# Fifteen small SBUF copies in a fused attention and MLP kernel, issued from ScalarE instead of SyncE

## The chip, the cores and the metric

The kernel runs on one core of a Trainium2 chip. The metric is the device time of one execution, in microseconds (us); runs of the kernel before and of the changed kernel are compared by their medians. Besides the runs there is one profiled execution of the kernel before, read through its profile: busy time by engine, a timeline of instructions, the chain of work that ended last, and the waits.

The engines are named as in the profile: PE is TensorE (matmuls), ACT is ScalarE, DVE is VectorE, POOL is GpSimd, SP is SyncE. SPq and ACTq stand for instructions that the sequencer of SP or of ACT carries out itself: DMA issues and separate semaphore waits.

## What is computed

One layer of 2048 positions and 448 channels: a windowed attention of 16 heads (28 channels each) in which each position looks at 8 earlier positions in steps of 2, and then a mixing MLP, each with a layer norm ahead and a residual.

```python
x = A_x
h = x + _A_ref(_layernorm(x), A_wqkv, A_wo)       # attention, 8 keys per query: idx = pos - 2*w
h2 = h + _B_ref(_layernorm(h), B_w1, B_w2, B_w3, B_w4)

# inside _A_ref
vg = v[:, :, idx_c, :].reshape(B, H, S, W, Dh)
logits = jnp.einsum("bhsd,bhswd->bhsw", q, kg) * scale
attn = _softmax(jnp.where(mask, logits, -1e9))
o = jnp.einsum("bhsw,bhswd->bhsd", attn, vg)
return o.reshape(B, S, D) @ wo
```

`_B_ref` multiplies the normalized input with w1, applies gelu, shifts four channel groups by -1, 1, -2 and 2 positions, multiplies with w2, adds the residual, normalizes again and applies a second two-layer MLP (w3, gelu, w4).

## The kernel before

The sequence is worked on in four blocks t = 0 to 3 of 512 positions. A block passes through phases: N1 (layer norm), A1 (q and k, transposed), V (v), A2 and S (logits by elementwise products on DVE and reducing matmuls on PE, then softmax), A3 (the weighted sum of v), O (output matmul and residual), B1 (norm and w1). The second half runs B2 (w2), W3 and B3 over units of 3, 4, 4, 4 and 1 tiles of 128 positions.

**How v reaches A3.** Phase V makes the v of a block in four matmul groups `il` = 0 to 3 of 128 positions, and ACT copies each from PSUM into `vt[:, sl, il, :]`, with `sl = t % 2`. A3 needs v in overlapping blocks: block j of `vw` holds 64 positions and the 16 ahead of them (`KW` = 80 partitions, `PADK` = 16). Since this moves data between partitions, it is done by DMA from `vt` to `vw`, four for each block (three for block 0, which has no predecessor):

- `vwp`: 16 partitions, the last rows of the block before; needs group 3 of block t - 1
- `vwa`: 64 partitions, the blocks with an even number; needs all four groups
- `vwb`: 80 partitions, the blocks with an odd number; needs all four groups
- `vwc`: 16 partitions, the padding of the other even blocks; needs groups 0 to 2

That makes 15 copies. `vw` and `vt` have two slots each, so block t overwrites what A3 of block t - 2 has read, and the `vt` of block t may be written only when the copies of block t - 2 have landed. A3 (matmuls `ps<-bd_r,vw` in the profile) reads them.

**What else is in SP's queue.** Every DMA is issued on SP: first the inputs and weights; then the copies of blocks 0 and 1; then the loads of w3 and w4 (`LOADS = '00'`: they wait for the landing of block 0's last copy); the copies of block 2; DMA transposes (`dma_turn`) of normalized data for B1 and B2, mixed with the copies of block 3; and the output.

**What sets the order.** The functions only describe operations, each with an engine, an assumed duration and its data. `_Sched.schedule` then simulates the engines by these durations and writes one fixed list of instructions for each engine. Among the operations of an engine that could start within a small slack (60 ns on ACT) of the earliest one, it takes the one with the lowest `prio`, that is, the one whose phase comes first in the string `PLAN` (line 13), and then the one described first. For a DMA, `dur` is the time for which the issuing engine is assumed to be taken, and `dma_land` is the latest planned landing; DMA transposes (planned with `nbytes` 0) are planned to start no earlier than 400 ns before it. `_emit_plan` works out the semaphore waits, which are emitted ahead of an instruction at line 1019; all instructions themselves are emitted at line 1021, so that the profile shows that line for nearly everything and an operation is known by its tiles. An operation also waits by semaphore for results of its own engine.

The names in the profile that matter here: `vt<-ps` (ACT, phase V), `vw<-vt` (the copies), `lntm<-xin` (ACT, in N1), `arena<-ps` (ACT, among others q and k of A1), `actT<-ps` (ACT, results of A3 and transposes), `xin<-ps` (ACT, phase O).

## Time and profile before

| | us |
|---|---|
| median of three runs | 202.25 (202.18 to 203.62) |
| the profiled execution, whole | 203.72 |
| its span, from the first to the last instruction | 202.0 |
| PE busy | 189.6 |
| DVE busy | 137.5 |
| ACT busy | 124.0 |
| POOL busy | 37.7 |

The profile comes from one execution, so durations and moments below are those of that execution; moments are counted in us from the start of its span. A busy PE is not PE at its peak, since matmuls are pipelined. ACT is busy for 61% of the span, but very unevenly, and the same holds for DVE. SP has no busy time in this count: issues and waits aren't counted. For an issue, the timeline's duration is the time in which the sequencer carried it out; "to landing" is the time from the issue to the arrival of the data.

```
DMA issues: out<-in engine op xcount, KB each, median us to landing
vw<-vt SPq DMA_DIRECT2D x4, 320.0 KB, 5.2      (vwb)
vw<-vt SPq DMA_DIRECT2D x4, 256.0 KB, 4.8      (vwa)
vw<-vt SPq DMA_DIRECT2D x4, 48.0 KB, 4.6       (vwc)
vw<-vt SPq DMA_DIRECT2D x3, 16.0 KB, 6.4       (vwp)
```

### The profile page before, as it was taken

The numbers are of one execution on the slowest core, as the hardware profiler recorded it, in microseconds if no ns is written. First come the engines' busy times: TensorE is split into PE (matmuls) and PEld (weight loads), VectorE is DVE, ScalarE is ACT, GpSimd is POOL, SyncE is SP. The second block draws the span as 40 slices with busy tenths as digits, with TensorE's granted clock in tenths as the row PEclk, the third lists the DMA queues.
The fourth block names the chain that finished last, engine by engine and source line by source line (L and its number), as shares of the span: only waits on it lengthen the run. The fifth ranks groups of instructions, "written<-read, shape, count | busy, mean of one in ns | idle before, by whom it ended". The sixth has DMA issues, their size and how long they took to land.

```text
span 202.0 us, 4020 instructions
## 1 busy us (share of the span) xinstructions
PE 189.6 (94%) x1638; PEld 92.4 (46%) x1638; DVE 137.5 (68%) x244; ACT 124.0 (61%) x270; POOL 37.7 (19%) x73
## 2 busy tenths in 40 slices
PE   6989994998989896899999999999999999999994
PEld 2454332444534453544455554445544455434553
DVE  6578999899899999986579998558112276013322
ACT  5938969988989999788974057960046610067000
POOL 6170000000000000990400180254000016201200
PEclk9999999999999999699999999999999999999999
DMA  5768689913413032005060000050600004300211
GB/s 160 246 195 176 161 199 334 263 61 82 94 28 75 7 78 54 3 0 104 3 127 0 23 28 0 4 103 23 149 26 0 0 0 86 89 23 0 49 49 45
DMA packets 25330, 15.89 MB, mean 79 GB/s; under 512 B 14064, under 2 KB 24800, under 8 KB 25312
## 3 DMA queue, kind: packets, MB, share of 16 engines
q1 hardware_dynamic: 25312, 15.63, 30.8%
q8 instruction: 13, 0.21, 0.4%
q14 instruction: 5, 0.04, 0.1%
HBM read 7.91 MB, written 1.84 MB: 48 GB/s over the span
## 4 chain that ended last, share of the span: by engine, by line
PE 72%; ACT 22%; POOL 1%; issue 1%; DMA 1%; DVE 1%; ACTq 0%; POOLq 0%
PE ps L1021 72%; ACT arena L1021 9%; ACT lntm L1021 4%; ACT actT L1021 3%; ACT xin L1021 1%; ACT nmr L1021 1%; DMA xin<-in_A_x_dram 1%; ACT rs_x L1021 1%; ACT vt L1021 1%; POOL ls L1021 1%; ACT L1021 1%; ACT ls L1021 1%; POOL arena L1021 0%; ACT rs_y L1021 0%; POOL zc L1021 0%
## 5 line engine op out<-in xcount | busy, mean ns | idle before, releaser
L1021 PE MATMUL ps<-actT,arena 128*128 128x512 bf16 (+4 forms) x348 | 68.1, 364 | 1.3 <-ACT vt L1021 0.8
L1021 ACT ACTIVATE arena<-ps 128x512 bf16<-128x512 f32 (+5 forms) x64 | 30.4, 528 | 23.6 <-PE ps L1021 23.1
L1021 PEld LDWEIGHTS ps<-actT,arena 128*128 128x128 bf16 (+1 forms) x348 | 27.5, 97 | 37.0 <-issue 8.2
L1021 PE MATMUL ps<-arena,h3T 128*128 128x448 bf16 (+1 forms) x238 | 43.9, 341 | 0.0
L1021 ACT ACTIVATE h3T<-ps 128x512 bf16<-128x512 f32 (+1 forms) x56 | 27.4, 586 | 26.4 <-PE ps L1021 26.4
L1021 DVE TENSOR_TENSOR qk_r<-arena 128x4096 bf16<-128x4096 bf16 (+1 forms) x16 | 32.4, 2064 | 1.9 <-PE ps L1021 1.8
L1021 PEld LDWEIGHTS ps<-arena,h3T 128*128 128x128 bf16 x238 | 23.2, 98 | 19.4
L1021 DVE SCALAR_TENSOR_TENSOR ost<-ps,mrs,arena 128x448 bf16<-128x448 f32 (+1 forms) x17 | 11.1, 655 | 24.7 <-PE ps L1021 24.5
L1021 POOL TENSOR_TENSOR arena<-arena,xin 128x448 f32<-128x448 f32 x16 | 18.3, 1170 | 41.6 <-ACT lntm L1021 27.1
L1021 ACT ACTIVATE actT<-ps 128x512 bf16<-128x512 f32 (+2 forms) x30 | 20.8, 725 | 8.4 <-PE ps L1021 8.4
L1021 POOL TENSOR_TENSOR rs_y<-rs_x,mhalf 128x4 f32<-128x4 f32 (+1 forms) x9 | 11.0, 1232 | 62.5 <-DVE rs_x L1021 62.5
L1021 DVE SCALAR_TENSOR_TENSOR arena<-xin,rs_y,ps 128x448 f32<-128x448 bf16 x16 | 10.6, 666 | 15.8 <-PE ps L1021 15.8
L1021 DVE TENSOR_TENSOR bd_r<-arena,bmask 80x2048 bf16<-80x2048 bf16 x16 | 18.7, 1210 | 0.0
L1021 PE MATMUL ps<-wo_s,actT 128*128 128x448 bf16 x64 | 15.5, 367 | 2.5 <-ACT actT L1021 2.5
L1021 DVE BATCH_NORM_STATS2 st<-xin 128x6 f32<-128x448 bf16 x24 | 14.7, 613 | 2.1 <-DMA xin<-in_A_x_dram 1.6
L1021 PE MATMUL ps<-w_s,arena 112*128 112x448 bf16 x64 | 13.8, 352 | 0.6 <-ACT arena L1021 0.6
L1021 PE MATMUL ps<-actT,w_s 128*112 128x512 bf16 (+1 forms) x64 | 14.0, 387 | 0.0
L1021 PE MATMUL ps<-arena,actT 128*128 128x448 bf16 (+1 forms) x64 | 12.2, 354 | 1.6 <-ACT actT L1021 1.6
L1021 PEld LDWEIGHTS ps<-wo_s,actT 128*128 128x128 bf16 x64 | 5.8, 100 | 8.4 <-ACT actT L1021 3.2
L1021 PEld LDWEIGHTS ps<-actT,w_s 128*112 128x112 bf16 (+1 forms) x64 | 6.5, 128 | 6.5 <-issue 2.4
L1021 PEld LDWEIGHTS ps<-w_s,arena 112*128 112x128 bf16 x64 | 6.0, 98 | 6.1 <-ACT arena L1021 0.7
L1021 PE MATMUL ps<-ident,lntm 128*128 128x128 bf16 x92 | 7.2, 231 | 1.5 <-DVE lntm L1021 1.5
(70 smaller groups left out, 173.8 us busy)
## 6 DMA issues: line engine op xcount, KB each, us to landing
out_dram<-ost SPq DMA_DIRECT2D x15, 112.0 KB, 1.7
arena<-in_B_w_dram SPq DMA_DIRECT2D x1, 1568.0 KB, 21.4
arena<-in_B_w_dram SPq DMA_DIRECT2D x1, 1344.0 KB, 7.7
vw<-vt SPq DMA_DIRECT2D x4, 320.0 KB, 5.2
vw<-vt SPq DMA_DIRECT2D x4, 256.0 KB, 4.8
xin<-in_A_x_dram SPq DMA_DIRECT2D x2, 448.0 KB, 10.5
xin<-in_A_x_dram SPq DMA_DIRECT2D x3, 224.0 KB, 4.6
arena<-in_A_wqkv_dram SPq DMA_DIRECT2D x1, 672.0 KB, 4.5
```

What stands on the lines that cost most here:

```text
L1021: inst = getattr(eng, meth)(**kw)
```

## The change

The copies are issued from ACT (`"act"`), each with an assumed 60 ns of the issuing engine in place of 650 ns, and the planned landing that holds back DMA transposes counts SP's DMAs only. The waits of each copy move with it. The sequence of all other instructions on each engine stays as it was.

```diff
@@ _Sched.schedule
                 if op.nbytes:
                     dma_free = max(st + op.dur, dma_free) + op.nbytes / dma_bw
                     op.t1 = dma_free + dma_fixed + op.lag
-                    dma_land = max(dma_land, op.t1)
+                    dma_land = max(dma_land, op.t1) if op.eng == "sp" else dma_land
@@ phase_V
             contract([group(il) for il in range(4)], ROUNDS["V"])
             if t > 0:
-                dma("vwp%d" % sl, vw[0:PADK, sl, 0, :], vt[112:128, 1 - sl, 3, :], PADK * 1024, 650.0)
-            dma("vwa%d" % sl, vw[PADK:KW, sl, 0:8:2, :], vt[0:64, sl, :, :], 64 * 4096, 650.0)
-            dma("vwb%d" % sl, vw[0:KW, sl, 1:8:2, :], vt[48:128, sl, :, :], 80 * 4096, 650.0)
-            last = dma("vwc%d" % sl, vw[0:PADK, sl, 2:8:2, :], vt[112:128, sl, 0:3, :], 16 * 3072, 650.0)
+                dma("vwp%d" % sl, vw[0:PADK, sl, 0, :], vt[112:128, 1 - sl, 3, :], PADK * 1024, 60.0, "act")
+            dma("vwa%d" % sl, vw[PADK:KW, sl, 0:8:2, :], vt[0:64, sl, :, :], 64 * 4096, 60.0, "act")
+            dma("vwb%d" % sl, vw[0:KW, sl, 1:8:2, :], vt[48:128, sl, :, :], 80 * 4096, 60.0, "act")
+            last = dma("vwc%d" % sl, vw[0:PADK, sl, 2:8:2, :], vt[112:128, sl, 0:3, :], 16 * 3072, 60.0, "act")
```

## The prediction

> **What bounds the kernel now.** I read the page first, then the chain of waits in order of time, then busy time by stretch, and last the timelines of SP and ACT around the copies. The chain ends in one long piece of PE:

> ```profile
> 34.50 7.09 PE ps L1021 x43
> ...
> 81.52 117.69 PE ps L1021 x789
> ```

> From 81.52 us on PE runs without a break, so the end moves with the moment at which PE gets there. Before it, the chain is PE from 12.97 to 27.75 and from 34.50 to 41.58, and otherwise mostly ACT. Busy time of that stretch, of the piece behind it, and of the rest:

> ```profile
> core 0: us, PE busy (x) PEld busy (x) DVE busy (x) ACT busy (x) POOL busy (x), PEclk, DMA share, GB/s
> 27.77:81.50 53.73, 46.62 (x690) 22.62 (x685) 50.74 (x75) 50.72 (x117) 0.64 (x2) 1.00 0.43 111
> 81.50:84.50 3.00, 2.98 (x16) 1.88 (x17) 3.00 (x2) 1.92 (x6) 3.00 (x2) 0.50 0.00 0
> ```

> ACT is busy for 50.72 of 53.73 us (94%) up to 81.5, although the page gives it 61% of the span. What is added to ACT here finds almost no idle time. The granted clock of 0.50 in the second row cost PE about 1.5 us (3 us at half speed); I come back to it.

> The copies on SP, and all of their issues in one row (min/median/max in ns):

> ```profile
> 21.54 5.96 SPq L1021 DMA_DIRECT2D vw<-vt  x7
> 28.45 3.20 SPq L1021 DMA_DIRECT2D arena<-in_B_w_dram  x3
> ...
> 41.99 8.46 SPq L1021 DMA_DIRECT2D vw<-vt  x4
> 58.60 2.00 SPq L1021 DMA_TRANSPOSE actT<-lntm  x1
> 66.62 7.91 SPq L1021 DMA_DIRECT2D vw<-vt  x4
> ...
> L1021 SPq DMA_DIRECT2D vw<-vt x15: 578/662/2625, 21.5 to 73.6; - x15
> ```

> ACT beside them:

> ```profile
> 21.79 0.62 ACT L1021 ACTIVATE lntm<-xin 128x448 bf16<-128x448 bf16 x1
> ...
> 24.03 1.88 ACT L1021 ACTIVATE vt<-ps 128x448 bf16<-128x448 f32 x4
> 27.77 1.58 ACT L1021 ACTIVATE arena<-ps 128x512 bf16<-128x512 f32 x3 [1.86 <-PE ps L1021]
> ...
> 48.92 0.60 ACT L1021 ACTIVATE actT<-ps 128x512 bf16<-128x512 f32 x1
> 49.40 0.56 ACT L1021 ACTIVATE xin<-ps 128x448 bf16<-128x448 f32 x1
> 50.73 0.55 ACT L1021 ACTIVATE xin<-ps 128x448 bf16<-128x448 f32 x1 [0.78 <-PE ps L1021]
> ...
> 70.71 2.13 ACT L1021 ACTIVATE actT<-ps 128x512 bf16<-128x512 f32 x4
> 73.25 0.55 ACT L1021 ACTIVATE xin<-ps 128x448 bf16<-128x448 f32 x1 [0.41 <-PE ps L1021]
> ```

> The brackets are the only idle time that ACT has near the copies: 1.86, 0.78 and 0.41 us, together 3.05.

> **What SP gains: nothing.** Nobody waits for SP behind the copies. The loads of w3 and w4 at 28.45 wait for the landing of block 0's last copy, which ACT would issue at the same moment as SP did; w3 lands 7.7 us after its issue and W3's first matmul is at 86.5, so that even some us of shift are covered by about 50 us. The transpose at 58.60 finds SP idle since 50.45 and waits for DVE's lntm. The data of the copies isn't waited for either: with the longest time to landing (9.2 us) block 0 is there by 33 and A3 reads it at 41.5; block 1, issued by 29.5, is read at 66.1; block 2, by 50.5, at 76.4; block 3, by 74.5, at 119. The vt slots are rewritten at 38.8 and 57.5, also after the landings. The line on the planned landing emits nothing, as the order stays: cost nil.

> **What ACT pays for one issue.** The trace holds no DMA issued from ACT. Bounds: ACT's separate semaphore waits take 17 to 38 ns each, SP's issues of these very copies 578 to 2625 ns. An issue can't shorten ACT's work, so there is no gain below nil. I take SP's durations copy by copy, since that is the same instruction on another sequencer; only the 2.62 us of the issue at 41.99 I replace by the median of 0.66, because SP's queue then still held the load of w4 (issued at 29.56, landing after 21.4 us), which isn't in ACT's queue.

> **What of it can hide.** ACT's sequencer runs ahead of the engine. The first eviction into a reused vt slot has four waits (its matmul, three landings), so it brings separate wait instructions; for block 3 they are recorded here:

> ```profile
> L1019 ACTq EVENT_SEMAPHORE  x3: 17/17/38, 54.5 to 55.0; - x3
> ...
> 57.50 1.80 ACT L1021 ACTIVATE vt<-ps 128x448 bf16<-128x448 f32 x4
> ```

> They are done at 54.5 to 55.0, the eviction starts at 57.5: a lead of 2.5 to 3.0 us, with three lntm and one ls in between. So an issue whose semaphores are met early costs ACT nothing while work is queued; one whose semaphore comes late stops the lead, and what stands behind it waits for its whole issue. [...]

> **Block 0 and 1 (7 issues).** By priority V 0 (9th in PLAN) stands before N1 3 (10th). So vwc, vwa, vwb follow the fourth vt eviction and come ahead of the lntm at 21.79. The first waits for ACT's own third eviction, which ended at 21.51; SP took from 21.54 to 23.74 for the three. The lntm starts at 23.76 instead of 21.79: +1.97. Behind it four lntm and block 1's four evictions shift as much; the third of those ends at 27.44 instead of 25.47. Its vwp is ready early and hides; vwc, vwa, vwb (25.50 to 27.50 on SP, 2.00 us) then run to 29.47. PE meanwhile needs the PSUM banks of these evictions for the last pass of A1 1: its weight loads were at 26.69, the evictions would end at 27.9 rather than 25.9, so its result comes at about 28.9 instead of 27.75. ACT is later: the arena eviction starts at 29.49 instead of 27.77. **+1.72**: 3.97 us of stops, less the idle 1.86 and rounding. From there the chain is ACT to 34.45, then PE to 41.58, so it is passed on in full.

> **Block 2 (4 issues).** Its priority (V 2, 27th) is behind everything ACT has then (A3 0, A1 2, O 0), so the issues go where the planner sees ACT free: between actT at 48.92 and xin at 49.40. vwp hides; the other three wait for A3 0's last matmuls (48.06 on SP) and take until 50.45, of which actT covers the first part. xin moves from 49.40 to 50.47, and the next xin, which follows 0.43 later, from 50.73 to 50.90. **+0.16**; the idle 0.78 is the cover, without it the cost is 1.07.

> **Block 3 (4 issues).** vwp lies ahead of the last actT and hides behind the table load and softmax. The rest stand between the last actT (72.24) and xin at 73.25, as V 3 (39th) comes before O 1 (45th). They wait for A3 1's last matmuls: 72.24 to 74.53. xin starts at 74.55: **+1.30**, and ACT then has no idle time up to the actT for which PE waits at 81.52.

> Sum: 1.72 + 0.16 + 1.30 = 3.2 us. Against the profiled execution that is 203.72 + 3.2 = 206.9 (its span 202.0 to 205.2, with the same 1.7 around it). That execution was 1.47 above the median of the runs, so I carry the sum to the median: 202.25 + 3.2 = 205.4.

> The half clock at 81.5 is the unknown beside it: PE's gaps shift against whatever sets it. If it vanishes the sum is 1.6 less, a second one costs as much more. I keep it, since the gaps ahead of 81.5 stay: 203.8 to 207.0 is the likeliest case's own range.

> **Rivals.**

> *The issue doesn't hold ACT.* If ACT's engine goes on with the instructions behind an issue, only the 17 to 38 ns of a wait remain, and the time is 202.3: not slower. It decides at 21.8: the lntm would start as before. For it: nothing on SP can show it, as SP does no other work. Against it: SP's issues never overlap (0.04 us lies between the end of one and the start of the next), so the sequencer itself is taken, and it must hand ACT each instruction. [...]

> *No lead.* If every issue stops ACT, vwp's included: all 15 durations are 12.6 us, 10.6 with 0.66 for the long one, less 3.05 of idle time: +7.6, 209.8. For it: copies that wait for ACT's own result end the lead each time. Against it: the wait records at 54.5.

> *The half clock goes away* beside my sum: 203.8, within 1%.

> *Faster.* No row gives 2 us: even no cost on ACT with no half clock is 200.6.

> **Numbers.** 1% of 202.25 is 2.0 us, about what measurements of this kernel can tell from no change; the bounds are 200.2 and 204.3. My forecast has 0.55, no lead 0.15, issue not holding 0.17, half clock gone 0.08, something unseen that is faster 0.05. Slower: 0.55 + 0.15 less 0.02 for the part of my own range under 204.3 = 0.68; within 1%: 0.17 + 0.08 + 0.02 = 0.27. The range takes in most of the not-holding case (from 202.2) and half of the no-lead case (to 209.5); outside lie 0.05, some 0.06 and some 0.08.

> **What would show it.** After the change ACTq has 15 DMA issues of about 0.65 us. Right if the lntm after the first four vt evictions starts about 2 us after the last of them, arena's 1.86 us idle before A1 1 now ends by ACTq, PE's wait at about 34.5 isn't longer than before by more than 1 us, and xin of O 1 starts after the third issue. Wrong if issues take under 0.1 us or activations run beside them; or if PE, not ACT, ends the waits up to 81.5, since then the sum is absorbed.

## The result, and the profile after

| | before | after |
|---|---|---|
| median of four runs each, us | 202.37 (202.18 to 203.62) | 211.79 (208.71 to 212.38) |
| ratio after to before | | 1.0325 [1.0239, 1.041] |
| the profiled execution, whole | 203.72 | 208.71 |
| its span | 202.0 | 207.0 |
| mean granted clock of the profiled execution | 0.992 | 0.984 |

The change makes the kernel slower by 3% (on the interval, 2.4 to 4.1%). The ratio is taken over fast runs alone, without 211.98 and 212.38; between the medians it is 1.047. The granted clock is the share of full speed at which PE was allowed to run, here as a mean over the execution. One run after took 208.71 us with a clock of 0.984, and three took 211.6 to 212.4 us with 0.966 or 0.967. The profile shows the first kind. The kernel before has two kinds as well: in runs shown further on it takes 202.2 to 202.6 us at clock 1.00 (0.998 and more), and about 204 us at 0.99.

The chain of waits after (start, duration, engine, tile):

```profile
22.39 0.70 ACTq L1021
...
23.12 0.64 ACTq L1021
...
23.81 0.58 ACT lntm L1021
...
36.98 8.67 PE ps L1021 x43
...
54.14 1.01 ACTq L1021
...
87.80 116.44 PE ps L1021 x789
```

ACTq, which the chain before did not have, now stands between two activations of ACT. PE's long piece starts at 87.80 us instead of 81.52. The timeline of ACT after, in the three places where copies are issued (a bracket is the engine's idle time and what the profile takes for its end):

```profile
20.66 1.43 ACT L1021 ACTIVATE vt<-ps 128x448 bf16<-128x448 f32 x3
21.68 2.08 ACTq L1021 DMA_DIRECT2D vw<-vt  x3
23.81 0.58 ACT L1021 ACTIVATE lntm<-xin 128x448 bf16<-128x448 bf16 x1 [1.72 <-issue]
24.14 0.58 ACTq L1021 DMA_DIRECT2D vw<-vt  x1
...
26.06 1.81 ACT L1021 ACTIVATE vt<-ps 128x448 bf16<-128x448 f32 x4
27.90 2.31 ACTq L1021 DMA_DIRECT2D vw<-vt  x3
30.26 1.58 ACT L1021 ACTIVATE arena<-ps 128x512 bf16<-128x512 f32 x3 [2.39 <-PE ps L1021]
```

```profile
52.14 0.57 ACTq L1021 DMA_DIRECT2D vw<-vt  x1
52.56 0.54 ACT L1021 ACTIVATE xin<-ps 128x448 bf16<-128x448 f32 x1
52.74 0.69 ACTq L1021 DMA_DIRECT2D vw<-vt  x1
52.98 0.60 ACT L1021 ACTIVATE actT<-ps 128x512 bf16<-128x512 f32 x1
53.47 1.68 ACTq L1021 DMA_DIRECT2D vw<-vt  x2
55.20 0.98 ACT L1021 ACTIVATE xin<-ps 128x448 bf16<-128x448 f32 x2 [1.61 <-PE ps L1021]
```

```profile
75.91 0.58 ACTq L1021 DMA_DIRECT2D vw<-vt  x1
76.06 1.66 ACT L1021 ACTIVATE actT<-ps 128x512 bf16<-128x512 f32 x3
77.12 2.37 ACTq L1021 DMA_DIRECT2D vw<-vt  x3
79.54 0.54 ACT L1021 ACTIVATE xin<-ps 128x448 bf16<-128x448 f32 x1 [1.82 <-PE ps L1021]
```

All 15 issues are there (569 to 1010 ns, median 670). After each group of three the next activation starts some 50 ns behind the last issue. Three of the brackets name PE wrongly. PE's timeline:

```profile
27.93 1.03 PE L1021 MATMUL ps<-actT,arena 64*128 64x512 bf16 x7 [0.47 <-ACT vt L1021]
...
52.75 0.35 PE L1021 MATMUL ps<-xin,ident 128*128 128x448 bf16 x1
...
77.73 0.35 PE L1021 MATMUL ps<-xin,ident 128*128 128x448 bf16 x1
...
79.13 0.35 PE L1021 MATMUL ps<-xin,ident 128*128 128x448 bf16 x1
```

The bank that xin reads at 79.54 was done by the matmul at 77.73 (its end is 78.09); the matmul at 79.13 belongs to the next bank. So xin could have started at about 78.1 and was held until 79.5 by the issues ahead of it. In the same way arena at 30.26 had its result from PE at 28.96, and xin at 55.20 had it at 53.10. None of the engines that compute waits for the landing of a copy in this profile, though the longest took 14.1 us.

The other part of the loss is the clock. PE's piece that starts at 36.98 lasts 8.67 us, where the same 43 instructions took 7.09. Busy time by stretch after (stretch, its length, PE busy, and so on; the granted clock is the number behind POOL's):

```profile
33.69:37.10 3.41, 1.19 (x17) 1.01 (x18) 3.31 (x7) 3.29 (x9) 0.00 (x0) 1.00 1.12 257
37.10:40.51 3.41, 3.41 (x18) 1.63 (x16) 3.41 (x2) 3.24 (x8) 0.00 (x0) 0.50 1.11 263
81.48:84.89 3.41, 0.92 (x65) 0.68 (x66) 3.41 (x4) 3.41 (x13) 0.00 (x0) 1.00 0.06 14
```

and the kernel before, in the stretch ahead of its one half clock:

```profile
77.76:81.17 3.41, 1.76 (x70) 0.99 (x69) 3.19 (x7) 3.41 (x10) 0.11 (x1) 1.00 0.01 2
```

After 84.89 the granted clock is 0.50 as well. In these two profiles half clock comes in stretches of 3.41 us: 37.10 to 40.51 and 84.89 to 88.30 after, 81.17 to 84.58 before. Ahead of each lies a stretch of the same length in which PE was busy for 1.19, 0.92 and 1.76 us: about half of it or less. PE's wait for the transposes ahead of 37.1 is 2.28 us in the profile after and 1.12 us before. First after:

```profile
34.27 1.07 PE L1021 MATMUL ps<-ident,lntm 128*128 128x128 bf16 x16 [2.28 <-DVE lntm L1021]
```

and before:

```profile
31.87 1.07 PE L1021 MATMUL ps<-ident,lntm 128*128 128x128 bf16 x16 [1.12 <-DVE lntm L1021]
```

So ACT's stops make PE wait longer there, and the second stretch of half clock follows; runs below test this.

**The account between the two profiled executions**, by where each instruction starts in both:

| place | us |
|---|---|
| ahead of the change (first vt eviction 18.14 to 18.28) | +0.14 |
| blocks 0 and 1 (arena 27.77 to 30.26, less that 0.14) | +2.35 |
| half clock at 37.1 (PE's piece 7.09 to 8.67) | +1.58 |
| block 2 (ACT's idle time at the two xin, 0.78 to 1.61) | +0.83 |
| block 3 (ACT's idle time at xin, 0.41 to 1.82) | +1.41 |
| the last piece of PE (117.69 to 116.44) | -1.25 |

The sum is 5.06, and the spans differ by 5.0. The last row is the half clock of before, which lay on the start of PE's long piece. After, the second stretch lies mostly ahead of that piece, on matmuls behind which PE had waited before: PE's piece starts 8.26 us behind the xin of O 1, and before it was 8.27 us, so this stretch cost almost nothing. The stops of ACT alone are 2.35 + 0.83 + 1.41 = 4.59.

### The profile page after: what moved, and what is told of

Same layout as the page of the kernel before. It is cut to its first block, busy times and chain, and to the rows that moved or that the text cites. A ratio compares the mean times of both kernels' runs of the same rounds, so it can differ in the third digit from the quotient of the medians.

```text
span 207.0 us, 4020 instructions
## 1 busy us (share of the span) xinstructions
PE 191.7 (93%) x1638; PEld 92.8 (45%) x1638; DVE 137.7 (67%) x244; ACT 124.2 (60%) x270; POOL 37.7 (18%) x73
## 3 DMA queue, kind: packets, MB, share of 16 engines
HBM read 7.91 MB, written 1.84 MB: 47 GB/s over the span
## 4 chain that ended last, share of the span: by engine, by line
PE 70%; ACT 22%; ACTq 3%; POOL 2%; issue 1%; DVE 0%; POOLq 0%
PE ps L1021 70%; ACT arena L1021 9%; ACT actT L1021 4%; ACT lntm L1021 3%; ACTq L1021 3%; ACT vt L1021 2%; ACT xin L1021 1%; ACT L1021 1%; POOL ls L1021 1%; ACT nmr L1021 1%; ACT ls L1021 1%; POOL arena L1021 0%; POOL zc L1021 0%; ACT rs_x L1021 0%; POOL ident L1021 0%
## 5 line engine op out<-in xcount | busy, mean ns | idle before, releaser
L1021 PE MATMUL ps<-actT,arena 128*128 128x512 bf16 (+4 forms) x348 | 68.3, 364 | 2.4 <-ACT vt L1021 1.9
L1021 ACT ACTIVATE arena<-ps 128x512 bf16<-128x512 f32 (+5 forms) x64 | 30.4, 528 | 25.6 <-PE ps L1021 25.1
L1021 PEld LDWEIGHTS ps<-actT,arena 128*128 128x128 bf16 (+1 forms) x348 | 27.4, 97 | 38.3 <-issue 8.6
L1021 PE MATMUL ps<-arena,h3T 128*128 128x448 bf16 (+1 forms) x238 | 43.9, 342 | 0.0
L1021 ACT ACTIVATE h3T<-ps 128x512 bf16<-128x512 f32 (+1 forms) x56 | 27.4, 588 | 26.3 <-PE ps L1021 26.3
L1021 DVE TENSOR_TENSOR qk_r<-arena 128x4096 bf16<-128x4096 bf16 (+1 forms) x16 | 32.4, 2064 | 2.2 <-PE ps L1021 2.0
L1021 PEld LDWEIGHTS ps<-arena,h3T 128*128 128x128 bf16 x238 | 23.2, 98 | 19.4
L1021 DVE SCALAR_TENSOR_TENSOR ost<-ps,mrs,arena 128x448 bf16<-128x448 f32 (+1 forms) x17 | 11.1, 656 | 24.7 <-PE ps L1021 24.5
L1021 POOL TENSOR_TENSOR arena<-arena,xin 128x448 f32<-128x448 f32 x16 | 18.3, 1170 | 43.0 <-ACT lntm L1021 28.5
L1021 ACT ACTIVATE actT<-ps 128x512 bf16<-128x512 f32 (+2 forms) x30 | 20.8, 726 | 7.4 <-PE ps L1021 7.3
L1021 POOL TENSOR_TENSOR rs_y<-rs_x,mhalf 128x4 f32<-128x4 f32 (+1 forms) x9 | 11.0, 1230 | 61.2 <-DVE rs_x L1021 61.2
L1021 DVE SCALAR_TENSOR_TENSOR arena<-xin,rs_y,ps 128x448 f32<-128x448 bf16 x16 | 10.6, 666 | 15.8 <-PE ps L1021 15.8
L1021 DVE TENSOR_TENSOR bd_r<-arena,bmask 80x2048 bf16<-80x2048 bf16 x16 | 18.8, 1212 | 0.3 <-ACT arena L1021 0.3
L1021 DVE BATCH_NORM_STATS2 st<-xin 128x6 f32<-128x448 bf16 x24 | 14.7, 613 | 4.0 <-ACT xin L1021 2.5
L1021 PE MATMUL ps<-wo_s,actT 128*128 128x448 bf16 x64 | 15.7, 371 | 1.3 <-ACT actT L1021 1.3
L1021 PE MATMUL ps<-arena,actT 128*128 128x448 bf16 (+1 forms) x64 | 13.4, 380 | 2.2 <-ACT actT L1021 2.2
L1021 PE MATMUL ps<-w_s,arena 112*128 112x448 bf16 x64 | 13.8, 352 | 0.6 <-ACT arena L1021 0.6
L1021 PE MATMUL ps<-actT,w_s 128*112 128x512 bf16 (+1 forms) x64 | 14.0, 387 | 0.0
L1021 PEld LDWEIGHTS ps<-actT,w_s 128*112 128x112 bf16 (+1 forms) x64 | 6.5, 128 | 6.5 <-issue 2.4
L1021 PE MATMUL ps<-ident,lntm 128*128 128x128 bf16 x92 | 6.6, 219 | 2.6 <-DVE lntm L1021 2.6
L1021 PEld LDWEIGHTS ps<-wo_s,actT 128*128 128x128 bf16 x64 | 5.8, 101 | 7.3 <-ACT actT L1021 2.0
L1021 POOL TENSOR_TENSOR mrs<-nm,rs_y 128x4 f32<-128x4 f32 x4 | 0.9, 233 | 44.4 <-ACT rs_y L1021 44.2
```

Of the source, the lines that this page charges most:

```text
L1021: inst = getattr(eng, meth)(**kw)
```

## The experiments

**Theory.** A DMA issue on ACT is carried out once every activation ahead of it has had its semaphores, and takes the sequencer 0.57 to 1.01 us in the profile after; activations that are already queued run on meanwhile, those behind the issue don't start. In the profile after, the issues behind an eviction of A3 begin 0.08 us after PE's matmuls for that eviction end (52.06 and 52.14, 75.83 and 75.91, 77.04 and 77.12). Where ACT's queue is empty by then, ACT stands still; these stops sum to 4.6 us. The rest is half clock, which the longer waits of PE bring on. **Rivals**: the second queue itself or the new times of the transfers cost the time; every issue costs ACT its 0.65 us wherever it stands; the stops of only one block carry all of it.

**One block at a time.** Only the copies of the named blocks are issued on ACT, the others on SP with their former planned cost:

```diff
+            cost, queue = (60.0, "act") if t in (0, 1) else (650.0, "sp")
-            dma("vwa%d" % sl, ..., 64 * 4096, 60.0, "act")
+            dma("vwa%d%s" % (sl, queue), ..., 64 * 4096, cost, queue)
```

The four dma calls are changed alike; the queue in the channel's name gives each queue its own semaphore. First, blocks 0 and 1:

> Only the 7 copies of blocks 0 and 1 are issued on ACT, the other 8 on SP as before. Theory (ACT stands behind the issues, and each block costs by itself): the two stops seen in the changed kernel's trace, 1.7 us behind block 0 and 2.3 us behind block 1, less the 1.9 us for which ACT waited for PE there anyway, so about +2.4 us: 204.8. With one further stretch of half clock (3.4 us long, costing up to 1.7) 206.4. Rival 1 (the copies on a second queue slow other transfers, wherever they are issued): most of the full slowdown, since the big loads of w3 and w4 run just then: 207 or more. Rival 2 (no cost of ACT's time, all of it clock): 202.4 where the granted clock is as before.

Measured: 207.02 us (206.21 to 208.51, 4 runs) against 203.82 (202.21 to 204.43, 19 runs), ratio 1.0185 [1.0115, 1.0254]. No run was at full clock: they had 0.991, 0.990, 0.983 and 0.975. ACT's stops are those of the whole change (the lntm starts at 23.69, arena at 30.17). More than expected, so the clock had to be taken out before the part could be priced (below).

Block 2 alone (`t in (2,)`):

> Only the 4 copies of block 2 are issued on ACT. Theory: the issues stand between actT and xin of O 0; in the changed kernel xin started 1.6 us after ACT fell idle where it had been 0, and 0.8 us of that were idle before too: +0.8, 203.2. My forecast's assumption that vwp hides would give +0.2, 202.5. Rival 1: small too, since no big load runs then, so this run tells only between 0.2 and 0.8.

Measured: 203.21 us (203.0 to 205.06, 10 runs), ratio 1.0014 [0.9975, 1.0053], so no difference is shown over all runs. Seven runs were at clock 1.00, at 203.0 to 203.31; eight of the 19 runs of before were, at 202.21 to 202.62. So block 2 costs about 0.8 us, and its three runs at 0.992 cost another 1.8.

Block 3 alone (`t in (3,)`):

> Only the 4 copies of block 3 are issued on ACT. Theory: xin of O 1 starts after the third issue, +1.4 us, and ACT has no idle time until PE waits for it: 203.8. If the half clock behind it shifts or falls partly into PE's waiting time, up to 1.3 us less: 202.5. Rival 1: nothing, no big load is under way and the data is read only 40 us later: 202.4.

Measured: 206.34 us (203.85 to 208.07, 4 runs), ratio 1.0102 [1.0014, 1.0191], at clocks 0.992, 0.983, 0.982 and 0.975: again more half clock than expected.

**All 15 on ACT, but later.** The same issues, moved in ACT's list to places where activations with met semaphores stand ahead of them; all other instructions keep their order:

```diff
+        def after_op(chan, nth, item, out, n):    # the nth copy of this channel goes behind
+            ...                                   # the nth activation of this item and tile
+            for seq in (order["act"], S.gorder):
+                seq.remove(mine)
+                seq.insert(seq.index(there) + 1, mine)
```

Block 0's go behind the four lntm of N1 3; block 1's (but for vwp, which stays) behind the third and tenth arena eviction of A1 1; block 2's behind an actT of A1 3 and the lntm of B1 0; block 3's behind the xin of O 2.

> All 15 copies stay on ACT's queue, but 14 of them are issued some activations later in ACT's order, behind activations whose semaphores are met by then, so that the engine has queued work for the time of the issues (block 0 behind the four lntm of N1 3, block 1 among the evictions of A1 1, block 2 behind the transposes' evictions and the lntm of B1 0, block 3 behind the last xin of O 2). Theory (only the stop behind an issue costs, not the queue it is on): most of the slowdown is gone, 202.4 to 203.4, with ACT's idle time in front of lntm and of xin back at the values of before. Rival 1 (the second queue or the transfers themselves): as slow as the changed kernel, 207 or more. Rival 3 (an issue always takes 0.65 us from ACT, also with work queued): about 15 x 0.65 less 3 us of idle time, 209.

Measured: 202.51 us (202.26 to 205.28, 10 runs), ratio 0.998 [0.9934, 1.0026]: no difference from before. Its timeline of ACT, first around block 0's, then around block 2's copies:

```profile
22.50 0.62 ACT L1035 ACTIVATE lntm<-xin 128x448 bf16<-128x448 bf16 x1
22.96 0.69 ACTq L1035 DMA_DIRECT2D vw<-vt  x1
...
23.06 0.61 ACT L1035 ACTIVATE lntm<-xin 128x448 bf16<-128x448 bf16 x1
```

```profile
53.33 1.02 ACT L1035 ACTIVATE actT<-ps 128x1024 bf16<-128x1024 bf16 x1
53.78 0.58 ACTq L1035 DMA_DIRECT2D vw<-vt  x1
54.25 1.02 ACT L1035 ACTIVATE actT<-ps 128x1024 bf16<-128x1024 bf16 x1
```

While the sequencer is in an issue, ACT goes from one activation to the next with no idle time. Fifteen issues on ACT's queue, most of them later than in the other versions, cost nothing that the interval shows. Both the second queue and a fixed price of an issue on the engine fall as causes.

**One copy earlier.** As block 2 alone, but its vwp is moved up in ACT's list past eleven activations (the expectation says ten), ahead of the activation that waits for A3 0's last matmuls:

> As the kernel with only block 2's copies on ACT, but vwp, the first of the four, moved 10 places up in ACT's order, right behind A3 0's second eviction, ahead of the activation that waits for A3 0's last matmuls. Theory (a DMA issue starts only when every activation ahead of it in ACT's order has had its semaphores, and that is why vwp of block 2 didn't hide): vwp is issued at about 44.4 beside queued activations, the next three start at 48.06, xin of O 0 at 50.5 instead of 51.2: 202.5 where the clock is 1.00, against 203.1 and 202.3 for that kernel and the kernel before. Rival (each issue costs ACT its 0.6 us wherever it stands): 203.1.

Measured: 203.13 us (202.29 to 204.31, 12 runs), ratio 1.0016 [0.9979, 1.0053]. Its seven runs at clock 0.998 to 1.00 have a median of 202.43, and the 17 runs of before at full clock beside them one of 202.28; the five others were at 0.992, which is why the median over all runs is near the rival's 203.1. Block 2 costs 0.15 us this way instead of 0.8, though one of the seven took 203.48. The timeline of ACT:

```profile
44.45 0.60 ACTq L1033 DMA_DIRECT2D vw<-vt  x1
44.53 0.66 ACT L1033 ACTIVATE actT<-ps 128x512 bf16<-128x512 f32 x1
...
48.12 0.73 ACTq L1033 DMA_DIRECT2D vw<-vt  x1
...
50.54 0.98 ACT L1033 ACTIVATE xin<-ps 128x448 bf16<-128x448 f32 x2 [0.91 <-issue]
```

vwp is out at 44.45, beside actT, and the other three begin at 48.12; at the same place of the list, some 4 us later, the changed kernel has vwp at 52.14. So in the changed kernel this copy, whose own data was long there, stood behind an activation that waited for PE.

**The clock taken out.** Some groups of matmuls and transposes in PE's gaps are issued two or three times in a row. They write the same result again, so that PE is busier in the waits; ACT, DVE and the DMAs are unchanged. For the changed kernel, some 4.8 us of them:

```diff
+REPEATS = [('A1 2', 'transpose', 0, 3), ('A1 2', 'transpose', 1, 2), ('O 1', 'matmul', 3, 2), ('A3 2', 'matmul', 1, 3), ('O 2', 'matmul', 0, 2)]
+        for item, eng_out, nth, times in REPEATS:
+            found = [op for op in order["pe"] if op.prio == place[item] and op.insts[0][0] == eng_out]
+            found[nth].insts = found[nth].insts * times
```

> The changed kernel with five groups of PE's matmuls done twice or three times over (same operands, same output; about 4.8 us of matmuls), placed where PE waits in its trace: the transposes at 34.3, the last O 1 group at 80.3, one A3 2 group at 83.6, the first O 2 group at 84.8. ACT's stops stay. Theory (what lies over the 3 us of ACT's stops is PE's clock: on a grid of 3.41 us, PE runs at half clock for the next 3.41 us after a stretch in which it was busy for about half or less): mean granted clock from 0.967 to 0.984 up to 0.985 to 1.00, time 205.3 to 207.2, the lower end where no half clock is left. The gap of 2.3 us ahead of the transposes can't be filled this way, so some runs keep one. Rival (the lost 8 us are all waiting behind ACT, the clock only follows): time unchanged at 208.7 to 212.4, or longer by the added matmuls.

Measured: 208.39 us (206.82 to 208.91, 6 runs) against 202.32 (202.16 to 205.41, 23 runs), ratio 1.0241 [1.0183, 1.03]. Two runs were at clock 1.00, at 206.82 and 206.84; the four others at 0.992. The median misses the expected range; at full clock the kernel takes 4.5 us more than before at full clock, which is the sum of ACT's stops.

The same on the kernel before (without the repeat in O 1, and the first transpose twice):

> The kernel before (all copies on SP) with four groups of PE's matmuls repeated in its two gaps (transposes at 31.9 twice, one A3 2 group at 77.3 three times, the first O 2 group at 78.5 twice; about 3 us of matmuls). Theory of the clock: the kernel before runs at 202.3 with a mean clock of 1.00 or at 204.1 with 0.99, by where the grid falls; with the gaps filled every run has 1.00 and 202.3 to 202.6. Rival: two kinds of runs as before, each up to 1 us longer.

Measured: 202.35 us (202.16 to 202.98, 12 runs), ratio 0.9981 [0.9951, 1.0011]. All 12 runs were at clock 0.999 or 1.00; of the 23 of before beside them, six were not and took 203.7 to 205.4. The transposes behind PE's wait in this kernel, and the busy time of the stretch around them:

```profile
32.38 1.96 PE L1025 MATMUL ps<-ident,lntm 128*128 128x128 bf16 x32 [1.12 <-DVE lntm L1025]
```

```profile
30.97:34.38 3.41, 2.25 (x34) 1.79 (x32) 3.31 (x10) 3.29 (x10) 0.00 (x0) 1.00 1.01 289
```

PE is busy for 2.25 of 3.41 us, 32 of its 34 instructions there are transposes, and no half clock follows. It is the quickest of all versions by the mean of its runs, but no gain in the median is shown.

**The parts at full clock.** Blocks 0 and 1 with repeats:

> Blocks 0 and 1 alone on ScalarE, with matmuls repeated in PE's gaps. Theory (this part costs the 2.35 us that ScalarE stood still, and the rest of its 207.0 us was the clock): runs at clock 1.00 come out at 204.6 to 205.0 us, and most runs are at 1.00. Rival (the issues cost PE more than the stops, by work that lands later): 206 us and more also at clock 1.00.

Measured: 205.78 us (204.78 to 206.84, 4 runs), ratio 1.0106 [1.0041, 1.0172]. Two runs at clock 1.00: 204.78 and 204.86, as the theory said; the two others were at 0.992, so that "most at 1.00" was missed. Block 3 with repeats:

> Block 3 alone on ScalarE, with matmuls repeated in PE's gaps. Theory (1.4 us of ScalarE, the rest of its 206.3 us was the clock): 203.6 to 204.0 us at clock 1.00, most runs there. Rival (the four issues cost more than ScalarE's stop): 205 us and more also at clock 1.00.

Measured: 203.61 us (203.49 to 204.16, 10 runs), ratio 1.0021 [0.9989, 1.0054]. All were at clock 0.998 or 1.00, nine of them at 203.49 to 203.91. With 202.3 for before at full clock, and medians of two, seven, ten and two runs (all but those of block 2 with repeats):

| copies on ACT | at full clock, us | over before | ACT's stops in the trace of after |
|---|---|---|---|
| blocks 0 and 1 | 204.8 | 2.5 | 2.35 |
| block 2 | 203.1 | 0.8 | 0.83 |
| block 3 | 203.6 | 1.3 | 1.41 |
| all | 206.8 | 4.5 | 4.59 |

The parts add up, and each is within 0.2 us of the stop that the trace shows.

**The changed kernel again**, for the spread of its time:

> The changed kernel once more, to see how its time is spread. Theory (ScalarE stops of 4.6 us plus one half-clock stretch of 3.41 us, worth up to 1.7 us, for each window of the clock's grid in which PE was busy half or less): no run below 206.8 us, which is what it took at full clock with the added matmuls; runs at clock 0.984 near 208.7, at 0.967 near 211.7; the product of span and clock stays at 203 to 204 us in all of them. Rival (the issues themselves take longer in the runs of 211 us): the product of span and clock rises with the time.

Measured: 210.19 us (208.48 to 211.82, 4 runs), ratio 1.0294 [1.0211, 1.0378]: 208.48 and 209.05 at clock 0.983 and 0.984, 211.34 and 211.82 at 0.966 and 0.967. The product of span and clock is 202.5 to 204.0 in all eight runs so far and does not rise with the time. That fits runs near 212 doing the same work at a lower clock.

> One look at the changed kernel again, for a profile of an execution at clock 0.967, if it falls so (4 of 8 so far did). Theory: the two stretches of half clock over those of the runs of 208.7 us follow windows of the clock's grid in which PE was busy half or less, in the waits that ScalarE's stops of block 1, 2 or 3 make longer, and lie before 88 us; the stops themselves are as before. Rival: they lie in the piece of PE after 88 us, which no wait of the change reaches.

> The same once more, in case the look before it falls at clock 0.984. Theory and rival as there.

Measured: 208.34 and 208.55 us, both at clock 0.983. In both, as in the other two profiles of this kernel, half clock begins at 36.6 to 37.6 and at 84.4 to 85.4. Of ten runs of the changed kernel five were near 208.6 and five near 211.8, and none of the second kind was caught with a profile. Where its other half clock lies stays open. Blocks 0 and 1 alone show one way: there the half clock that began at 36.10 lasted 6.83 us, twice the usual:

```profile
36.10:39.51 3.41, 2.61 (x13) 1.63 (x14) 3.41 (x3) 3.15 (x6) 0.00 (x0) 0.50 1.11 251
39.51:42.92 3.41, 3.41 (x12) 0.96 (x11) 2.19 (x3) 3.41 (x12) 0.00 (x0) 0.50 0.77 198
```

**Which runs get half clock.** The stretches of half clock fit a grid with a step of 3.41 us, whose position changes from run to run (last section). For each kernel's one profile one can estimate which share of these positions puts a window with PE busy for 0.42 or less (in brackets: 0.52 or less) on one of PE's waits between 20 and 95 us; both bounds are read from the profiled executions, as the last section has them. For before, block 2 alone, the later placement and vwp ahead the share is 0.31 (0.51 to 0.52), and of the 88 runs of these four in the experiments 37 were below 0.998. For the changed kernel and for blocks 0 and 1 alone it is every position, and all 14 runs were. For before with repeats and block 3 with repeats it is none, and none of 22 runs was. In between lie block 3 alone with 0.67 (0.90) and four of four runs, the changed kernel with repeats with 0.44 (0.64) and four of six, and blocks 0 and 1 with repeats with 0.59 (0.79) and two of four. So in these runs the longer waits turn a half clock that comes by chance into one that always comes. The four profiles of the changed kernel lie close together on the grid, within 0.93 us, which may be why none shows a run near 212.

## Why the prediction was right or wrong

The direction was right, and so was the mechanism of ACT's stops; what the forecast said of the clock was not. The range of 202.2 to 209.5 held the profiled execution (208.71) but not the median (211.79); the ratio of 1.0325 puts the changed kernel at 208.9, inside it. Of the 9.4 us between the medians, 4.5 are ACT's stops, forecast at 3.2. The rest, 4.9, goes with the clock, which the forecast kept as it was; for the runs near 212 this rests on their mean clock, as no profile shows one.

**The signs.** The lntm came behind the issues and xin of O 1 behind the third, as named. PE's wait at about 34.5 grew only from 1.56 to 1.65 us, also as named, but the one ahead of it, which no sign covered, from 1.12 to 2.28. Arena's idle time is put down to PE by the profile, though its result was there at 28.96.

**What SP gains: nothing.** Right: the account between the two profiles needs no term for SP, and none of the engines that compute waited for a copy's landing.

**The price of one issue, from SP's rows.** Right: 569 to 1010 ns with a median of 670, against the 0.66 taken.

**Block 0 and 1, +1.72.** Right in kind: the lntm starts at 23.81, forecast 23.76, and the first vwp of block 1 hides at 24.14. PE's result for arena came at 28.96, forecast 28.9, and ACT was later, as said. The term was too small: 2.35. The failing step is "vwc, vwa, vwb (25.50 to 27.50 on SP, 2.00 us) then run to 29.47". In block 1 vwc is the last of the three, so all of them wait for the fourth eviction (27.87) and not the third, and they take 2.31 us. The working's "3.97 us of stops, less the idle 1.86 and rounding" is 2.11 and not 1.72; the 0.39 between them is no rounding but the part of the issues that was taken to run beside the fourth eviction.

**Block 2, +0.16.** The failing step is "vwp hides". It was issued at 52.14, behind the actT that waits for PE's matmuls at 51.64, and pushed the three others back by 0.6 us, when these alone used up the cover of 0.78:

```profile
51.64 0.42 PE L1021 MATMUL ps<-bd_r,vw 80*32 80x64 bf16 x32
```

With vwp moved ahead the block costs 0.15: the remainder of the term was right.

**Block 3, +1.30.** Measured 1.41 in the trace and 1.3 by runs at full clock.

**The half clock: "I keep it, since the gaps ahead of 81.5 stay".** This step failed, and it is the larger part of the miss. The gaps don't stay: PE's waits at 34.3 and 37.0 became 2.28 and 1.65 us, where before they were 1.12 and 1.56, and a stretch with PE busy for 1.19 of 3.41 us was the result. The prediction priced one more stretch at 1.6 (measured 1.58) but did not ask what sets it, so that the runs with more than two stretches lay outside its range (a mean clock of 0.967 over 210 us is worth about four of them, an estimate from the runs). Carrying the sum to the median hid a part of it: the median run of before was, by its time, one at full clock, and the 1.47 us between it and the profiled execution was that one stretch. For the same reason the 1.6 us that the rivals of 203.8 and 200.6 take off for a half clock that goes away weren't in the median.

**The rival that the issue doesn't hold ACT** was half true. Activations that were queued before the issue run on, which the later placement shows at its full extent (202.51); those behind it don't start. The trace of after shows it at the lntm of 23.81: it had a free engine from 22.09 on, and in the kernel before it started as soon as ACT was free, but here it came only after the third issue. **No lead** fell: vwp at 24.14 is issued beside an lntm with seven more activations (three lntm, four evictions of vt) ahead of the issue in ACT's list and not yet begun.

## What to carry to other kernels

Fifteen DMA issues on ACT's queue cost nothing that the interval shows (ratio 0.998 [0.9934, 1.0026]) where 14 of them stood behind activations that were ready, and 4.5 us at full clock in the changed kernel, where after each group of three ACT stood idle until the last issue was done. What ACT would have idled anyway came off: at xin of block 2 it was idle for 1.61 us, of which 0.78 were there before. So look at what stands ahead of each issue, not only at whether its own data is there. Move such issues behind ready activations before giving up the queue. When a change makes PE's gaps longer, count the clock as a cost of its own (here 4.9 of the 9.4 us between the medians go with it): read the granted clock of every run and compare runs of equal clock before pricing a part.
